# First batch of an attention and maxout kernel: key sums with ones as stationary operand, agent values divided on VectorE, product evacuated by VectorE, fillers moved

## The chip, the cores and the metric

The kernel runs on one core of one Trainium2 chip. The metric is the device time of one execution in microseconds (us), lower is better. The kernel before takes 467.8 us (median of three runs, 466.63 to 468.07).

## The reference

Agent attention in four batches, then a feed-forward layer with a maximum of three products. For each batch b (12544 rows of 128 channels, 49 agents):

```python
scale = 1.0 / np.sqrt(q.shape[-1])
a2k = softmax(scale * agents @ k.T)     # 49 x 12544, over the keys
agent_v = a2k @ v                       # 49 x 128
q2a = softmax(scale * q @ agents.T)     # 12544 x 49, over the agents
x = q2a @ agent_v
h = np.maximum(np.maximum(x @ w1, x @ w2), x @ w3)   # 768 columns
out = h @ w_out
```

The inputs are float32 in HBM, and the output is float32, 50176 x 128.

## The kernel before

The product of agent_v with the weights (w2 - w1, w3 - w1 and so on) is taken once per batch and kept as G, so a slice of 1024 query rows needs only its exps e_q and G. Slices and the k groups of the next batch are interleaved over 49 steps. The first batch has no slices to hide behind: its twelve groups of k and v (ten of nine tiles of 128 rows, two of four) are read, turned (transposed on TensorE), scored and summed by themselves. Evacuating means copying a result of TensorE out of the memory that it writes to (the tiles `uv_ps`, `m_ps` and `o_ps`); a hidden tile is 128 of the 768 hidden columns for one slice. `C31` and `C21` are the places in G where the parts for w3 - w1 and w2 - w1 begin. Every operation is put down with a key, `at(key, ...)`, and is emitted in the order of the keys, so the order of each engine is fixed by hand. The kernel also runs *fillers*, matmuls whose result nobody uses, to keep TensorE busy.

The parts that the change touches (cuts marked):

```python
    def keep_busy(times):                                   # a block of fillers
        t = small_tile("m_ps")
        for _ in range(times):
            nc.tensor.matmul(t, ident, busy, start=True, stop=True, skip_group_check=True)
    # ... in k_group(b, t0, n, key, s); early = first batch
        def values():
            t, c = (d["pair"][:, 1, :], 0) if early else (d["s"], CV)
            for j in range(n):
                e = d["e"][:, j, :A] if early else d["e"][:, j * A:(j + 1) * A]
                nc.tensor.matmul(t[:, c:c + A], d["vb"][:, j, :], e, start=(early and j == 0),
                                 stop=True, skip_group_check=True)

        def key_sums():                                     # exps stationary, one column of ones moving
            for j in range(n):
                for h in range(2):
                    nc.tensor.matmul(d["pair"][h * H:(h + 1) * H, 1, A:A + 1], d["e"][:, j, :],
                                     ones_bf[:, :1], start=False, stop=True, skip_group_check=True)
    # ... in k_tail: the sums' reciprocal scales G when it is evacuated
        def normalise():
            src = last_tile["v"][:, A:A + 1] if s is None else host[s][:, :1]
            nc.vector.reciprocal(r_ag[:, b:b + 1], src)
    # ... in product(c0, *ends), after the matmuls of a piece
                if s is None and c0 == C31:
                    nc.vector.tensor_scalar_mul(G[b][:, a:z], src, r_ag[:, b:b + 1])
                else:
                    nc.scalar.activation(G[b][:, a:z], src, AF.Copy, scale=r_ag[:, b:b + 1])
    # ... in q_group, first slice
            at(last_key + 0.76, turn_q, ("qt", 0), (), "om", [("qe", 0)])
            at(last_key + 0.77, evacuate, ("qe", 0), [("qt", 0)])
            at(last_key + 0.96, scores, ("s", 0), [("qe", 0)], "om", [("ex", 0)])
            at(last_key + 0.97, exps, ("ex", 0), [("s", 0)])
    # ... where the first batch's groups are put down
        if 4 <= g < len(first_sizes) - 2:
            fillers += [(first_key + 6.0 * g + 0.55, 3), (first_key + 6.0 * g + 1.3, 3)]
    k_tail(0, last_key, (last_key + 0.95, last_key + 1.02), None)
    for key, n in fillers + [(KEY["u3"] + 0.05, 2)]:
        at(key, lambda n=n: keep_busy(n), ("busy", key), (), "om", [("busy", key)])
```

The softmax here doesn't subtract the row's maximum and nothing guards it: scores larger than these inputs give would overflow.

## Time and profile before

| | |
|---|---|
| median of the runs | 467.8 us |
| span of the profiled execution | 466.1 us, mean granted clock 0.993 |
| TensorE busy | 442.2 us (95%) |
| VectorE, ScalarE busy | 402.3 (86%), 397.2 us (85%) |
| first batch (loads, scores, values) | 0 to about 44 us |
| thin stretch with the halved clock | about 46 to 53 us |
| steady part | about 66 us to the end |

The prediction shows the lines. In them PE is TensorE's matmuls and PEld its weight loads, DVE is VectorE, ACT ScalarE, POOL GpSimd. A row of the chain of waits reads: start, length, what ended the wait.

### The profile page before, as it was taken

The numbers are of one execution on the slowest core, as the hardware profiler recorded it, in microseconds if no ns is written. First come the engines' busy times: TensorE is split into PE (matmuls) and PEld (weight loads), VectorE is DVE, ScalarE is ACT, GpSimd is POOL, SyncE is SP. The second block draws the span as 40 slices with busy tenths as digits, with TensorE's granted clock in tenths as the row PEclk, the third lists the DMA queues.
The fourth block names the chain that finished last, engine by engine and source line by source line (L and its number), as shares of the span: only waits on it lengthen the run. The fifth ranks groups of instructions, "written<-read, shape, count | busy, mean of one in ns | idle before, by whom it ended". The sixth has DMA issues, their size and how long they took to land.

```text
span 466.1 us, 13549 instructions
## 1 busy us (share of the span) xinstructions
PE 442.2 (95%) x5566; PEld 277.8 (60%) x5573; DVE 402.3 (86%) x514; ACT 397.2 (85%) x461; POOL 171.4 (37%) x179
## 2 busy tenths in 40 slices
PE   2598999999999999999999999999999999999996
PEld 2576456666665666666656766666656555555554
DVE  4254689999989999999989999999988999999995
ACT  3364788999999989899898899998999999999992
POOL 3245855364353453644362536444150010100000
PEclk9999799999999999999999999999999999999999
DMA  8999999998999999996998999996946668643222
GB/s 321 408 409 393 410 336 303 272 342 177 315 302 259 300 323 299 319 293 146 300 334 304 275 310 304 278 295 169 186 125 176 165 167 164 170 136 112 71 85 98
DMA packets 81449, 118.26 MB, mean 254 GB/s; under 512 B 55207, under 2 KB 56683, under 8 KB 81387
## 3 DMA queue, kind: packets, MB, share of 16 engines
q1 hardware_dynamic: 81184, 117.30, 84.0%
q8 instruction: 43, 0.70, 0.6%
q14 instruction: 19, 0.16, 0.1%
q10 hardware_dynamic: 203, 0.10, 0.1%
HBM read 78.74 MB, written 25.69 MB: 224 GB/s over the span
## 4 chain that ended last, share of the span: by engine, by line
PE 84%; DVE 5%; ACT 4%; DMA 4%; issue 2%; SPq 0%; POOL 0%; DVEq 0%; ACTq 0%; POOLq 0%
PE uv_ps L544 34%; PE o_ps L583 28%; PE o_ps L574 6%; DVE r L569 4%; PE m_ps L497 4%; PE m_ps L518 3%; ACT a_sb L559 3%; DMA st<-in_k_dram 2%; PE m_ps L257 2%; DMA st<-in_v_dram 2%; PE m_ps L332 1%; PE m_ps L315 1%; PE uv_ps L297 1%; PE m_ps L532 1%; PE uv_ps L338 1%
## 5 line engine op out<-in xcount | busy, mean ns | idle before, releaser
L569 DVE TENSOR_TENSOR r<-uv_ps,a_sb 128x1024 bf16<-128x1024 f32 x245 | 297.1, 1219 | 16.0 <-PE uv_ps L544 6.2
L559 ACT ACTIVATE a_sb<-uv_ps 128x1024 bf16<-128x1024 f32 x245 | 240.8, 1027 | 14.4 <-PE uv_ps L544 12.9
L544 PE MATMUL uv_ps<-e_q,G 49*128 49x512 bf16 (+3 forms) x1248 | 187.9, 370 | 2.7 <-DVE r L569 0.6
L583 PE MATMUL o_ps<-wo_bf,r 128*128 128x128 bf16 x2352 | 175.3, 220 | 0.2 <-DVE r L569 0.2
L583 PEld LDWEIGHTS <-r 128*128 128x128 bf16 x2352 | 137.8, 98 | 40.0 <-issue 38.1
L544 PEld LDWEIGHTS <-G 49*128 49x128 bf16 x1248 | 57.8, 94 | 65.3 <-issue 32.9
L358 POOL TENSOR_TENSOR Eacc<-Eacc,e_k 128x441 f32<-128x441 f32 (+1 forms) x30 | 30.5, 1015 | 132.6 <-ACT e_k L326 132.6
L590 DVE TENSOR_TENSOR o_sb<-o_ps,recips 128x512 f32<-128x512 f32 x98 | 67.4, 688 | 8.9 <-PE o_ps L583 6.3
L492 POOL CAST q_bf<-st 128x1024 bf16<-128x1024 f32 x49 | 50.8, 1040 | 60.8 <-DMA qT<-q_bf 59.5
L567 ACT ACTIVATE r<-uv_ps 128x1024 bf16<-128x1024 f32 x49 | 50.1, 1023 | 17.7 <-PE uv_ps L544 17.4
L283 POOL CAST k_bf<-st 128x1152 bf16<-128x1152 f32 (+2 forms) x45 | 50.5, 1122 | 27.5 <-DMA st<-in_k_dram 24.9
L556 ACT ACTIVATE uv_ps<-uv_ps 128x1024 f32<-128x1024 f32 x49 | 49.6, 1012 | 2.6 <-PE uv_ps L544 2.4
L574 PE MATMUL o_ps<-G,e_q 128*128 128x256 bf16 x196 | 38.0, 276 | 0.6 <-DVE o_sb L590 0.6
L290 POOL CAST v_bf<-st 128x1152 bf16<-128x1152 f32 (+1 forms) x33 | 37.4, 1134 | 0.7 <-DMA st<-in_v_dram 0.3
L524 ACT ACTIVATE e_q<-m_ps 128x512 bf16<-128x512 f32 x49 | 29.8, 607 | 1.4 <-PE m_ps L518 1.4
L303 DVE COPY kT<-uv_ps 128x1152 bf16<-128x1152 bf16 (+1 forms) x15 | 10.7, 712 | 18.1 <-PE uv_ps L297 18.0
L574 PEld LDWEIGHTS <-e_q 128*128 128x128 bf16 x196 | 12.5, 97 | 19.3 <-issue 17.8
L288 ACT ACTIVATE v_bf<-st 128x1152 bf16<-128x1152 f32 (+1 forms) x12 | 12.8, 1070 | 13.0 <-DMA st<-in_v_dram 12.9
L497 PEld LDWEIGHTS <-q_bf 128*128 128x128 bf16 x264 | 15.3, 99 | 12.9 <-issue 11.6
L503 DVE COPY qT<-m_ps 128x1024 bf16<-128x1024 bf16 (+1 forms) x33 | 22.2, 672 | 0.8 <-PE m_ps L497 0.8
L497 PE MATMUL m_ps<-ident,q_bf 128*128 128x128 bf16 x264 | 20.9, 223 | 0.0
L518 PE MATMUL m_ps<-qT,agT 128*64 128x512 bf16 (+3 forms) x104 | 19.9, 388 | 0.0
(73 smaller groups left out, 219.9 us busy)
## 6 DMA issues: line engine op xcount, KB each, us to landing
st<-in_q_dram SPq DMA_DIRECT2D x46, 512.0 KB, 4.8
out_dram<-o_sb SPq DMA_DIRECT2D x46, 512.0 KB, 3.5
st<-in_k_dram SPq DMA_DIRECT2D x40, 576.0 KB, 6.0
st<-in_v_dram SPq DMA_DIRECT2D x40, 576.0 KB, 7.1
st<-in_k_dram SPq DMA_DIRECT2D x3, 512.0 KB, 6.0
st<-in_v_dram SPq DMA_DIRECT2D x3, 512.0 KB, 6.8
wst<-in_moe_w_dram SPq DMA_DIRECT2D x3, 384.0 KB, 10.4
st<-in_q_dram SPq DMA_DIRECT2D x2, 384.0 KB, 4.2
```

Of the source, the lines that this page charges most:

```text
L283: nc.gpsimd.tensor_copy(out=d["kb"][:, :n, :], in_=d["k"][:, :n, :])
L290: nc.gpsimd.tensor_copy(out=d["vb"][:, :n, :], in_=d["v"][:, :n, :])
L492: nc.gpsimd.tensor_copy(out=d["qb"], in_=d["q"])
L497: nc.tensor.transpose(t[:, j * P:(j + 1) * P], d["qb"][:, j, :], ident)
L544: nc.tensor.matmul(t[:, h, j0 * P:j1 * P], G[b][h * H:h * H + A, col + f * P:col + (f + 1) * P], d["e"][h * H:h * H + A, j0 * P:j1 * P], s ...
L556: nc.scalar.activation(u, u, AF.Relu)
L559: nc.scalar.activation(a_sb[f], u, AF.Relu)
L567: nc.scalar.activation(r, v_ps[f], AF.Relu)
L569: nc.vector.tensor_tensor(out=r, in0=v_ps[f], in1=a_sb[f], op=ALU.max)
L574: nc.tensor.matmul(t[:, i * 2 * C:(i + 1) * 2 * C], d["e"][:, jj * P:(jj + 1) * P], G[batch[jj]][:, C1O:C1O + 2 * C], start=(i == 0), stop ...
L583: nc.tensor.matmul(t[:, c:c + C], r_sb[f][:, h, jj * P:(jj + 1) * P], wo_bf[:, f, :], start=False, stop=True, skip_group_check=True)
L590: nc.vector.tensor_tensor(out=d["out"][:, j:j + m, :], in0=d["o", o].rearrange("p (j c) -> p j c", c=C), in1=d["r"][:, j:j + m].unsqueeze( ...
```

## The change

Its intent is to shorten the ramp ahead of the steady part. The sums of the exps come from a matmul with ones as stationary operand and the exps moving, so every partition holds the sum of each agent in one row of 49; half as many matmuls are needed, and the division can be done once on the agent values (128 x 49) in place of on G. G's pieces are then plain copies, all on VectorE. The scores of the first q slice come ahead of the product. The turn of the next batch's first k group goes behind the second hidden tile. Six fillers near the end of the batch go, and four come in the thin stretch.

```diff
-                last_tile["v"] = d["pair"][:, 1, :]
+                last_tile["t"] = d["s"]
 ...
-                e = d["e"][:, j, :A] if early else d["e"][:, j * A:(j + 1) * A]
+                e = d["e"][:, j * A:(j + 1) * A]
                 nc.tensor.matmul(t[:, c:c + A], d["vb"][:, j, :], e, start=(early and j == 0),
                                  stop=True, skip_group_check=True)
-        def key_sums():
-            (cut: the 2 n one-column matmuls above)
-        def add_sums():
-            (cut)
+                if early:
+                    nc.tensor.matmul(t[:, A:2 * A], ones_bf, e, start=False, stop=True,
+                                     skip_group_check=True)
 ...
-                turn = 6.0 * s - 3.3 if s else KEY["u1"] + 0.01
+                turn = 6.0 * s - 3.3 if s else KEY["v0"] + 0.01
 ...
         def normalise():
-            src = last_tile["v"][:, A:A + 1] if s is None else host[s][:, :1]
-            nc.vector.reciprocal(r_ag[:, b:b + 1], src)
+            if s is None:
+                r = last_tile["t"][:, :A]
+                nc.vector.reciprocal(r, Vacc[b][:, A:])
+                nc.vector.tensor_tensor(out=avT[:, b, :A], in0=Vacc[b][:, :A], in1=r, op=ALU.mult)
+            else:
+                nc.vector.reciprocal(r_ag[:, b:b + 1], host[s][:, :1])
 ...
-                if s is None and c0 == C31:
-                    nc.vector.tensor_scalar_mul(G[b][:, a:z], src, r_ag[:, b:b + 1])
+                if s is None:
+                    nc.vector.tensor_copy(out=G[b][:, a:z], in_=src)
 ...
-            at(last_key + 0.96, scores, ("s", 0), [("qe", 0)], "om", [("ex", 0)])
-            at(last_key + 0.97, exps, ("ex", 0), [("s", 0)])
+            at(last_key + 0.94, scores, ("s", 0), [("qe", 0)], "om", [("ex", 0)])
+            at(last_key + 0.941, exps, ("ex", 0), [("s", 0)])
 ...
-        if 4 <= g < len(first_sizes) - 2:
+        if 4 <= g < len(first_sizes) - 3:
             fillers += [(first_key + 6.0 * g + 0.55, 3), (first_key + 6.0 * g + 1.3, 3)]
 ...
-    for key, n in fillers + [(KEY["u3"] + 0.05, 2)]:
+    for key, n in fillers + [(last_key + 0.9, 2), (KEY["u1"] + 0.01, 2),
+                             (KEY["u3"] + 0.05, 2)]:
```

Cut are the tiles and arguments that follow from it (no ones behind the exps, Vacc 98 columns wide, no scale when the linear part of G is evacuated).

More of the change, by code (lines that the diff above doesn't have):

```diff
@@ L174 @@
     r_ag = const.tile([P, B], FP32, name="r_ag")
-    e_first = [const.tile([P, KT, H], BF16, name=f"e_first{i}") for i in range(3)]
-    for t in e_first:
-        nc.vector.memset(t[:, :, A:], 1.0)
     sel = const.tile([P, 2], BF16, name="sel")
@@ L251, in linear_product_out @@
     def linear_product_out():
-        nc.scalar.activation(G[0][:, C1O:WC], linear["t"][:, C:3 * C], AF.Copy, scale=r_ag[:, 0:1])
+        nc.scalar.activation(G[0][:, C1O:WC], linear["t"][:, C:3 * C], AF.Copy)
     def keep_busy(times):
@@ L318, in exps @@
         def exps():
-            if early:
-                d["e"] = e_first[early_groups.index(t0) % 3]
-                nc.scalar.activation(d["e"][:, :n, :A],
-                                     d["s"][:, :n * A].rearrange("p (j a) -> p j a", a=A), AF.Exp,
-                                     scale=scale)
-                return
             d["e"] = work.tile([P, KT * A], BF16, tag="e_k", bufs=3, name="e_k")
@@ L330, in values @@
             for j in range(n):
-                e = d["e"][:, j, :A] if early else d["e"][:, j * A:(j + 1) * A]
+                e = d["e"][:, j * A:(j + 1) * A]
                 nc.tensor.matmul(t[:, c:c + A], d["vb"][:, j, :], e, start=(early and j == 0),
                                  stop=True, skip_group_check=True)
-        def key_sums():
-            for j in range(n):
-                for h in range(2):
-                    nc.tensor.matmul(d["pair"][h * H:(h + 1) * H, 1, A:A + 1], d["e"][:, j, :],
-                                     ones_bf[:, :1], start=False, stop=True, skip_group_check=True)
-        def add_sums():
-            src = d["pair"][:, 1, A:A + 1]
-            nc.vector.tensor_tensor(out=src, in0=src, in1=Vacc[b][:, A:], op=ALU.add)
+                if early:
+                    nc.tensor.matmul(t[:, A:2 * A], ones_bf, e, start=False, stop=True,
+                                     skip_group_check=True)
         def add_values():
-            w = A + 1 if early else A
+            w = 2 * A if early else A
             src = d["pair"][:, 1, :w] if early else d["s"][:, CV:CV + A]
-            if t0 + n == NT:
-                nc.vector.tensor_tensor(out=avT[:, b, :A], in0=src[:, :A], in1=Vacc[b][:, :A], op=ALU.add)
+            if t0 + n == NT and not early:
+                nc.vector.tensor_tensor(out=avT[:, b, :A], in0=src, in1=Vacc[b], op=ALU.add)
             elif t0:
@@ L378, in k_group @@
             at(min(key + 13.2, done), values, ("kv", g), [("ke", g)])
-            at(min(key + 13.2, done), key_sums, ("kn", g), [("kv", g)])
-            at(min(key + 13.6, done + 0.01), add_values, ("ka", g), [("kv", g), ("kn", g)])
-            if t0 + n == NT:
-                at(done + 0.02, add_sums, "sums0", [("ka", g)])
+            at(min(key + 13.6, done + 0.01), add_values, ("ka", g), [("kv", g)])
         else:
@@ L445, in k_tail @@
         at(sum_key + 0.81, normalise, ("normalise", b),
-           ["sums0"] if s is None else [("total", s), ("ka", s - 1)])
+           [("ka", ("early", NT - last_size))] if s is None else [("total", s), ("ka", s - 1)])
         pieces = ((C31, C31 + 2 * P, C1O) if s is None else (C31, WC), (C21, C31))
@@ L672 @@
     last_size = first_sizes[-1]
-    early_groups = [sum(first_sizes[:g]) for g in range(len(first_sizes))]
     at(first_key - 35, prep, "prep", (), "om", ["prep"])
```

## The prediction

> **What bounds the kernel now.** I read the page first, for the share of each engine and the strip of slices.
>
> ```profile
> PE 442.2 (95%) x5566; PEld 277.8 (60%) x5573; DVE 402.3 (86%) x514; ACT 397.2 (85%) x461; POOL 171.4 (37%) x179
> ...
> PE   2598999999999999999999999999999999999996
> ...
> PEclk9999799999999999999999999999999999999999
> ```
>
> TensorE is the bound, and its row is full from slice 3 on. Only the first slices have holes, and the granted clock dips in one of them (slice 4, 46.6 to 58.3 us). Next I cut the span into stretches with the table of windows (columns: length, busy time with count for PE, PEld, DVE, ACT, POOL, then clock, DMA share, GB/s).
>
> ```profile
> 26.00:42.00 16.00, 15.74 (x328) 12.00 (x330) 8.24 (x16) 9.43 (x14) 7.13 (x7) 1.00 1.04 398
> 42.00:44.50 2.50, 1.77 (x48) 1.48 (x42) 1.01 (x4) 0.73 (x3) 0.85 (x1) 1.00 1.03 410
> 44.50:47.00 2.50, 1.52 (x12) 0.73 (x13) 1.57 (x4) 1.05 (x3) 2.20 (x3) 0.85 1.01 406
> 47.00:50.00 3.00, 2.65 (x15) 1.24 (x16) 0.82 (x2) 2.71 (x3) 2.91 (x4) 0.50 1.03 409
> 50.00:54.00 4.00, 3.87 (x36) 1.98 (x36) 2.58 (x3) 1.78 (x3) 3.22 (x4) 0.61 1.02 409
> ...
> 66.00:400.00 334.00, 332.45 (x4189) 208.34 (x4188) 312.56 (x384) 307.28 (x357) 138.13 (x142) 1.00 0.92 258
> ```
>
> From 66 us PE is busy 332.45 of 334: nothing to gain there without taking PE work away. The order of instructions of both kernels, compared with line numbers stripped, is the same after about 62 us. So the change can only move the date at which the steady part starts. Before that date, 26 to 42 us is full of PE work, part of it fillers (matmuls whose result nobody uses) and all beside a saturated DMA (398 to 410 GB/s); 42 to 54 us is a thin stretch in which the clock falls to 0.50. The chain of waits shows what is serial there.
>
> ```profile
> 41.74 0.38 PE uv_ps L338 x18
> 42.12 0.32 PE uv_ps L315 x8
> 42.44 0.33 ACT e_first L321
> ...
> 43.29 0.57 PE m_ps L497 x8
> ...
> 43.88 0.33 DVE qT L503
> ...
> 44.26 0.22 DVE avT L349
> ...
> 44.91 0.18 DVE r_ag L418
> ...
> 45.18 0.49 DVE G L437
> ...
> 46.38 0.61 ACT e_q L524
> ...
> 48.06 1.08 PE uv_ps L297 x9
> ```
>
> The end of the first batch runs scores, exps, values, agent values (avT), reciprocal, product into G, then the first slice's exps (e_q) and hidden matmuls. The last row is nine transposes in 1.08 us; the same nine took 0.50 us at 37.41. That is the halved clock.
>
> **What the Trainium skill says.** (1) "TensorE: Matmul & The Clock Gate", Part 1, "The HAM clock gate": the clock is 1.2 GHz by default and 2.4 GHz after a busy window of about 3.4 us, and falls back after an idle one; the windows run freely. The trace agrees on the ratio (1.08 against 0.50 us) and roughly on the time: it is slow from about 46.2 to 53 us, 6.8 us, or two windows. It also shows that a thin stretch is enough: PE was 61% busy in 44.5 to 47. (2) Same page, "Back-to-back issue gap": start to start never under about 25 ns however small N is. Nine values matmuls of 49 columns take 0.23 us in the chain, 25.6 ns each; but the 18 one-column ones take 0.38 us, 21 ns each, slightly under it. So a one-column matmul costs nearly what a 49-column one does. (3) "VectorE: DVE Perf Modes", "First, the fixed hardware budget": reciprocal repeats a divide step 8 times. That might mean 8 cycles per element; the groups by shape say less.
>
> ```profile
> L538 DVE RECIPROCAL recips<-m_ps 128x8 f32<-128x8 f32 x49 | 9.7, 197 | 0.1
> L418 DVE RECIPROCAL r_ag<-m_ps 128x1 f32<-128x1 f32 x3 | 0.5, 168 | 3.4 <-PE m_ps L413 3.4
> ```
>
> Seven more elements cost 29 ns, 4.1 ns each, so 49 elements should take about 0.168 + 48 x 0.0041 = 0.37 us.
>
> **The change part by part.**
>
> Key sums. Removed: 18 matmuls of one column per group of nine tiles (0.38 us). Added: nine of 49 columns with ones stationary (estimate 0.23 us, as for the values). Saved: 0.15 us per group, 0.15 x 98/9 = 1.6 us over the batch. It all lies on PE, which is the chain from 21 us to 42 us, but only as far as data have arrived (below).
>
> Fillers before the end of the batch. The group ten from the start loses its two blocks of three: 0.22 + 0.38 at 37.9 and 0.75 at 39.38 in the chain, 1.35 us of PE time. With the sums, PE could finish some 2.4 us sooner from 26 us on.
>
> How far data allow it. POOL's casts wait for loads:
>
> ```profile
> 38.96 0.61 POOL L283 CAST k_bf<-st 128x512 bf16<-128x512 f32 x1 [0.71 <-DMA st<-in_k_dram]
> 40.90 1.04 POOL L492 CAST q_bf<-st 128x1024 bf16<-128x1024 f32 x1 [1.33 <-DMA st<-in_q_dram]
> ```
>
> The last k group is ready at 39.57 and the first q slice at 41.94. PE turns q between the last two values groups, in program order, at 43.29 now; it cannot before about 42.0. DMA is saturated, so these dates don't move. So of the 2.4 us, about 1.25 us survive: qT's evacuation starts at 42.6 in place of 43.88.
>
> The division. Before: avT sum (0.21) starts at 44.26, then sum column and reciprocal (0.17 each) run beside the product matmul; G's evacuation starts 0.92 us after avT started. After: sum (about 0.26 for 98 columns), reciprocal 0.37, multiply 0.21, each waiting for the one ahead (0.03 to 0.24 us a hop, as between 44.26 and 44.91), then matmul and start of evacuation, about 0.35. Sum 1.25 to 1.6: longer by 0.3 to 0.7 us. So G's first piece ends at 44.8 to 45.3 in place of 45.66.
>
> The exps of q move ahead of the product (they now end near 44.7, before 46.99), so they leave the chain. But the hidden matmuls still stand behind all product matmuls on PE (about 1.2 us after G's first piece), so they start near 46.1, 0.9 us sooner than 47.03.
>
> Product evacuated by VectorE: ACT loses 0.90 us (46.98) which stood ahead of the first relu, so relu starts when the first hidden matmul is done, 46.6 in place of 47.78. VectorE gains about 0.48, 0.75 and 1.02 (slope 0.27 us per 256 columns), where it had idled 2.26 us.
>
> Turning k behind the second hidden tile and four more fillers (two ahead of q's scores, two after the first two hidden tiles, 0.43 us a pair at full clock, 0.85 at half): if the clock stays up, transposes, hidden tiles and q's turn save about 2 us of PE time between 47 and 52; the relus then bind and the fourth hidden tile starts at 49.2 rather than 51.5. Gain 2.3 us. If the clock still drops, the fillers cost nearly what they fill, and the gain shrinks to 0.3 to 0.8 us.
>
> I can't tell which. The change also thins PE at 40 to 45 us (data-bound, fillers gone): by my timetable it is busy for about half of 40.3 to 45.2. I give a full clock 45%. Mean: 0.45 x 2.3 + 0.55 x 0.6 = 1.4 us, so 467.8 - 1.4 = 466.4.
>
> **The rivals.** (a) The clock drops earlier, at 43 us, because the batch's end is thinner: the chain of serial hops at half clock gives all the lead back, 467.5 to 468.2. For it: 61% busy was too little before. Against: two fillers stand in the hole. (b) VectorE becomes the bound of the first slices: its three copies take 2.25 us in a row and the second hidden half waits for the third. For it: that wait is new. Against: ACT needs until 48.5 for two relus anyway. It costs under 1 us: about 466. (c) The lead is lost later, to loads for the next batch: DMA share is 1.02 until 62 us. Against: casts run 3 us or more ahead of the transposes that use them. Then 467.5. (d) All works and the clock stays up: 465.
>
> **Range and chances.** (d) and (a) set the ends, with 0.5 us for the scatter of the runs before (466.63 to 468.07): 464.6 to 468.2. 2% would be 9.4 us, four times the best case: faster 0.01, slower 0.01, same 0.98.
>
> **What the profile after would show.** Nine values and nine sums in about 0.46 us in the chain; qT's evacuation near 42.6; the 49-wide reciprocal near 0.37 us; the first relu near 46.6; and PE fuller and nine transposes in 0.5 us at 47 to 52 (d) or 1.1 us (a). From 66 us to the end, the same length as before within 0.5 us. I am wrong if the steady part changes length, if the last q load lands at another time, or if the clock behaves in a third way.

## The result, and the profile after

The changed kernel takes 464.55 us (median of four executions, 464.44 to 464.77). The ratio to the kernel before is 0.9936, 95% interval 0.9919 to 0.9953: same by the limit of 2%, but clearly 0.6% faster. The four executions of the kernel before in that comparison took 466.63 to 468.07; the experiments below have 33 more. A ratio is the mean time of one kernel's fast runs over that of the other's of the same rounds, so it is not quite the ratio of the medians.

The strip of the page after, as before: the dip of the clock in slice 4 is gone.

```profile
PE 438.5 (95%) x5473; PEld 274.3 (59%) x5473; DVE 402.8 (87%) x512; ACT 396.5 (86%) x460; POOL 171.1 (37%) x179
...
PE   2597899999999999999999999999999999999995
...
PEclk9999999999999999999999999999999999999999
```

The table of windows after, same columns as in the prediction:

```profile
42.00:44.50 2.50, 1.58 (x21) 0.85 (x19) 1.64 (x5) 1.15 (x2) 0.80 (x1) 1.00 1.02 410
44.50:47.00 2.50, 2.26 (x17) 0.78 (x16) 1.61 (x3) 1.33 (x3) 2.18 (x3) 1.00 1.02 407
47.00:50.00 3.00, 2.52 (x34) 1.63 (x33) 2.30 (x3) 1.69 (x3) 2.94 (x4) 1.00 1.02 410
50.00:54.00 4.00, 3.51 (x39) 1.69 (x39) 3.31 (x6) 3.91 (x6) 3.19 (x4) 1.00 1.03 409
66.00:400.00 334.00, 332.96 (x4178) 207.91 (x4175) 312.43 (x386) 307.60 (x357) 136.90 (x142) 1.00 0.88 260
```

From 44.5 to 47 TensorE is busy for 2.26 us of 2.5 in place of 1.52, and the clock stays at 1.00 in all stretches. The steady part looks as before.

The chain of waits after (start, length, what):

```profile
40.64 1.05 POOL q_bf L478
...
41.74 0.64 PE m_ps L483 x8
...
42.40 0.44 DVE qT L489
...
44.13 0.43 DVE G L423
...
45.80 0.39 PE uv_ps L530 x2
...
47.06 0.62 PE uv_ps L294 x9
```

Its start is new: GpSimd's cast of the first q slice, which waited for the load, has taken the place of TensorE's backlog. Nine transposes take 0.62 us in place of 1.08. Point by point:

| event | before | after | gain |
|---|---|---|---|
| q's load has landed, cast starts | 40.90 | 40.64 | 0.26 |
| evacuation of qT starts | 43.88 | 42.40 | 1.48 |
| first piece of G done | 45.66 | 44.55 | 1.11 |
| first hidden matmuls start | 47.03 | 45.28 | 1.75 |
| first relu starts | 47.78 | 45.71 | 2.07 |
| in-place relu of the fourth hidden tile starts | 52.13 | 48.96 | 3.17 |
| first output scaled | 64.91 | 61.71 | 3.20 |
| end | 466.1 | 462.7 | 3.4 |

Nearly all is won by 52 us and kept. From the first scaled output to the end it is 401.2 us before and 401.0 after.

### The profile page after: what moved, and what is told of

Same layout as the page of the kernel before. It is cut to its first block, busy times and chain, and to the rows that moved or that the text cites. A ratio compares the mean times of both kernels' runs of the same rounds, so it can differ in the third digit from the quotient of the medians.

```text
span 462.7 us, 13350 instructions
## 1 busy us (share of the span) xinstructions
PE 438.5 (95%) x5473; PEld 274.3 (59%) x5473; DVE 402.8 (87%) x512; ACT 396.5 (86%) x460; POOL 171.1 (37%) x179
## 4 chain that ended last, share of the span: by engine, by line
PE 80%; DMA 8%; DVE 5%; ACT 4%; issue 1%; SPq 0%; POOL 0%; DVEq 0%; ACTq 0%
PE uv_ps L530 34%; PE o_ps L569 29%; PE o_ps L560 6%; DMA st<-in_k_dram 5%; PE m_ps L483 4%; DVE r L555 4%; PE m_ps L504 3%; ACT a_sb L545 2%; DMA st<-in_q_dram 2%; DMA st<-in_v_dram 2%; PE m_ps L323 2%; PE m_ps L312 1%; PE m_ps L518 1%; DVE o_sb L576 1%; ACT e_q L510 0%
```

## The experiments

Twelve kernels ran, each five rounds and a profiled execution (six executions); the kernel before, 33 in all. All gave correct results. "Full" counts executions whose mean granted clock over the whole span was 0.996 or more. What lies between 0.996 and 1.000 is not the thin stretch in the traces that we have: e0's, at 0.997, shows 1.00 up to 460 us and 0.61 from there, where the last work of TensorE ends. The last two columns are a ruler from the one trace of each: from the start of q's cast (so the landing of q's load, which varies between 40.33 and 41.38, is taken out) to the first scaled output, and from there to the end.

| run | edit | median (lowest to highest) | full | q cast to first output | to the end |
|---|---|---|---|---|---|
| before | | 467.39 to 467.58 in the three calls (465.93 to 469.3) | 18 of 33 | 24.01 | 401.2 |
| after, first runs | whole change | 464.55 (464.44 to 464.77) | 4 of 4 | 21.07 | 401.0 |
| e0 | whole change | 464.63 (464.38 to 465.73) | 6 of 6 | 21.08 | 401.1 |
| e1 | less the new fillers | 465.96 (464.53 to 467.45) | 1 of 6 | 23.73 | 400.8 |
| e2 | before, new fillers alone | 466.65 (466.03 to 467.62) | 6 of 6 | 24.03 | 401.2 |
| e7 | sums and division alone | 466.90 (465.10 to 468.31) | 2 of 6 | 21.39 | 401.1 |
| e11 | sums, division, new fillers | 465.17 (464.58 to 466.46) | 5 of 6 | 21.40 | 401.4 |
| e3 | second piece of G by ScalarE | 464.96 (464.47 to 465.46) | 6 of 6 | 21.23 | 401.1 |
| e4 | turn of k early again | 465.10 (464.59 to 465.59) | 6 of 6 | 21.11 | 401.4 |
| e5 | old fillers kept | 464.64 (464.21 to 464.74) | 6 of 6 | 21.09 | 401.1 |
| e6 | before, old fillers dropped | 467.18 (465.73 to 468.41) | 1 of 6 | 23.08 | 401.1 |
| e8 | values ahead of q's turn | 464.55 (463.45 to 465.37) | 6 of 6 | 20.42 | 401.3 |
| e9 | e8, one old filler pair less | 464.24 (463.65 to 465.34) | 5 of 6 | 20.49 | 400.8 |
| e10 | e9, q's cast split | 464.06 (463.79 to 464.74) | 5 of 6 | 20.57 | 400.8 |

The executions of the kernel before fall in groups by their own mean clock: 14 at 0.998 or 0.999 take 466.6 us on average (median 466.4), 11 at 0.991 take 468.4, and 8 between them 467.4. So a full dip costs about 1.8 us. By this reckoning the kernel before has one in a third of its executions and perhaps part of one in another quarter; only one trace of it was kept, so where the clock fell in the others is not shown. The average of all 33 is 467.4, 0.8 above the full-clock ones. The ten executions of the changed kernel (first runs and e0) average 464.7. The gain is thus about 1.9 us at equal clock and about 0.8 us of dips that no longer come, 2.7 us together.

### e0: the change again

```diff
(none)
```

> The changed kernel once more, as the yardstick for the runs beside it. Both theories: 464.5 us (464.2 to 465.0), clock near 1.00. If some of its executions show a clock near 0.99 and take 466 us or more, the full clock in its first trace was luck of the phase.

Measured 464.63 us, all six executions at 0.997 or more. The full clock in the first trace was no luck. One execution at 0.999 took 465.73; no trace shows why.

### e1: without the new fillers

```diff
-    for key, n in fillers + [(last_key + 0.9, 2), (KEY["u1"] + 0.01, 2),
-                             (KEY["u3"] + 0.05, 2)]:
+    for key, n in fillers + [(KEY["u3"] + 0.05, 2)]:
```

> The changed kernel without its two new pairs of fillers (4 matmuls of 512 columns, about 0.9 us of TensorE at full clock). Theory 'clock': without them the clock falls again near 43 to 47 us and stays low for two windows; time 466.0 to 467.2, mean clock about 0.99. Rival 'dates': the gain is the removed work and the new order; time 464.2 to 464.8, as less TensorE work is left.

Measured 465.96 us; the one execution at 0.999 took 464.53, as the whole change does, the others 464.86 to 467.45 at 0.989 to 0.995. The table of windows of its profiled execution:

```profile
42.00:44.50 2.50, 1.03 (x17) 0.68 (x16) 1.70 (x5) 1.19 (x2) 1.15 (x1) 1.00 1.02 406
44.50:47.00 2.50, 1.89 (x16) 0.57 (x13) 1.55 (x2) 1.59 (x2) 2.35 (x3) 0.75 1.03 409
47.00:50.00 3.00, 2.78 (x20) 2.04 (x21) 1.91 (x3) 0.34 (x1) 2.92 (x4) 0.50 1.02 409
50.00:54.00 4.00, 3.88 (x41) 2.07 (x40) 2.01 (x3) 3.30 (x4) 3.21 (x4) 0.50 1.03 408
54.00:58.00 4.00, 3.82 (x29) 1.26 (x28) 3.64 (x5) 3.42 (x6) 2.91 (x5) 0.75 1.02 411
```

TensorE is busy 1.03 us from 42 to 44.5 in place of 1.58, and then the clock falls to 0.50. It stays there from about 45.8 to 56 us, 10.2 us, where it was 6.8 us in the trace before. Four matmuls without a use are worth 1.3 us on average, all of it through the clock as far as one execution can show: the one at full clock without them took neither more nor less. 'Clock' is confirmed; its range, from 466.0, is missed by 0.04 us, and the low stretch is longer than it forecast.

### e2: the new fillers alone

```diff
+    for key, n in fillers + [(last_key + 0.9, 2), (KEY["u1"] + 0.01, 2),
+                             (KEY["u3"] + 0.05, 2)]:
-    for key, n in fillers + [(KEY["u3"] + 0.05, 2)]:
```

> The kernel before with only the two new pairs of fillers added. Theory 'clock': the clock stays full at 46 to 53 us and 1.2 to 2.0 us are gained: 465.8 to 466.6. Rival 'dates': nothing is gained, 467.6 to 468.4, as the fillers add 0.9 us to TensorE.

Measured 466.65 us, all executions at 0.996 or more: the dips are gone, as 'clock' says (0.05 above its range), and 466.65 is what the kernel before takes at full clock. The gain in the same rounds is 0.15% with an interval that includes none (0.9964 to 1.0006). Half of its executions took 466.0 to 466.2 and the others 467.1 to 467.6. The profiled one is of the second kind, and its casts on GpSimd show where that came from:

```profile
20.86 1.15 POOL L283 CAST k_bf<-st 128x1152 bf16<-128x1152 f32 x1 [5.93 <-DMA st<-in_k_dram]
```

The same cast in the kernel before:

```profile
19.86 1.15 POOL L283 CAST k_bf<-st 128x1152 bf16<-128x1152 f32 x1 [4.65 <-DMA st<-in_k_dram]
```

One load came 1 us later, and q's turn then starts at 44.34 in place of 43.22, although q itself had landed at 40.39. With the old sums TensorE works off a backlog from 21 us to the end of the batch, so a late load at 20 us was not made good in this trace.

### e7: sums and division alone

```diff
(shortened: the change, with fillers, turn of k, order of q's scores as before, and)
+                if s is None and c0 == C31:
+                    nc.vector.tensor_copy(out=G[b][:, a:z], in_=src)
+                elif s is None:
+                    nc.scalar.activation(G[b][:, a:z], src, AF.Copy)
```

> Only the new key sums with the division on VectorE: product's second part evacuated by ScalarE, fillers, turn of k and order of q's scores as before. Theory 'clock': lead of about 0.15 us x 7 groups at the end of the batch, less 0.3 us for the longer division, and the clock still falls: 467.0 to 467.6. Rival 'dates': the sums are the larger part of the gain: 465.5 to 466.5.

Measured 466.90 us: above the rival's range and 0.1 below the theory's. The two full executions took 465.10 and 465.91, the three at 0.988 or 0.989 took 467.5 to 468.3. Its trace is of a full one: q's turn at 41.94, when the cast ended at 41.89. The turn follows the values matmuls without a gap, so the sums alone bring TensorE's own work level with q's load (with the old fillers dropped too, it waits 0.56 us for the cast in the changed kernel). At full clock that is most of the gain; but without new fillers the clock fell in four of six executions, and hides it. That this is more often than before rests on e1, e6 and e7 together (14 of 18, against 15 of 33 in the kernel before); e7 alone does not show it. The expectation had the size of the lead right and its worth too low.

### e11: sums, division and new fillers

```diff
(e7, with the new fillers)
```

> The new sums and division (as in e7) and the two new pairs of fillers, nothing else. Theory 'data limit and clock': those two carry nearly all of the gain: 464.9 to 465.4 in every execution, mean clock 0.997 or more. Rival: VectorE's evacuation, the later turn of k or the order of q's scores carry a large part, or keep the clock up: 466 or more, or executions near 467 at 0.99.

Measured 465.17 us, 5 of 6 at full clock, those five 465.08 on average. Of the 1.9 us at equal clock (466.6 to 464.7) the sums carry 1.5. By the ruler 0.33 us is left for all other parts (21.40 against 21.07). The theory holds for the median; of the single executions, one at 0.994 took 466.46, and one at 1.000 took 464.58, less than it allowed.

### e3: second piece of G on ScalarE

```diff
+                if s is None and c0 == C31:
+                    nc.vector.tensor_copy(out=G[b][:, a:z], in_=src)
+                elif s is None:
+                    nc.scalar.activation(G[b][:, a:z], src, AF.Copy)
-                if s is None:
-                    nc.vector.tensor_copy(out=G[b][:, a:z], in_=src)
```

> The changed kernel with the product's second part (768 columns) evacuated by ScalarE again. Theory: it stands ahead of the first relu (0.9 us from about 45.4), so the relus start near 46.3 in place of 45.71 and 0.4 to 0.7 us are lost: 464.9 to 465.3. Rival: the relus are not on the chain, or VectorE's copy costs as much elsewhere: 464.3 to 464.7.

Measured 464.96 us, against 464.64 of e5, which by its own result below is as good as the whole change; by the ruler 0.16 us. ScalarE in time order:

```profile
45.28 0.81 ACT L425 ACTIVATE G<-uv_ps 128x768 bf16<-128x768 f32 x1 [0.84 <-PE uv_ps L418]
...
45.99 1.94 ACT L547 ACTIVATE a_sb<-uv_ps 128x1024 bf16<-128x1024 f32 x2
```

The relu starts at 45.99, only 0.28 us later than in the changed kernel (45.71), where it waits for the first hidden matmuls. A small part of the gain, at the low end of the range expected (464.9).

### e4: turn of k early

```diff
-                turn = 6.0 * s - 3.3 if s else KEY["v0"] + 0.01
+                turn = 6.0 * s - 3.3 if s else KEY["u1"] + 0.01
```

> The changed kernel with the turn of the next batch's k back ahead of the second hidden tile. Theory: the turn then takes the product's second buffer (free at 46.6) and the second hidden tile that of the first relu (46.7), so the two only change places: 464.4 to 464.9. Rival: the relus or VectorE's maximum wait longer: 465.2 or more.

Measured 465.10 us, above the theory's range and below the rival's. The trace shows no loss ahead of the first output (21.11 against 21.07); from there to the end it takes 401.4 in place of 401.0 to 401.1, but e8 shows 401.3 without this edit, and e7, which turns k early too, 401.1. So whether the order of the turn costs anything stays open.

### e5 and e6: the old fillers near the end of the batch

```diff
e5, in the changed kernel:
-        if 4 <= g < len(first_sizes) - 3:
+        if 4 <= g < len(first_sizes) - 2:
e6, in the kernel before:
-        if 4 <= g < len(first_sizes) - 2:
+        if 4 <= g < len(first_sizes) - 3:
```

> The changed kernel with the two blocks of three fillers of the tenth group put back (1.35 us of TensorE). Theory 'data limit': with the new sums TensorE already waits for k and q, so q's turn still starts at about 41.8 and the time stays 464.4 to 464.9, full clock. Rival 'TensorE backlog': the fillers are on the chain and cost up to 1.3 us: 465.5 to 466.

Measured 464.64 us. The cast and turn of q in its trace:

```profile
40.42 1.04 POOL L478 CAST q_bf<-st 128x1024 bf16<-128x1024 f32 x1 [1.38 <-DMA st<-in_q_dram]
...
41.54 0.27 PE L483 MATMUL m_ps<-ident,q_bf 128*128 128x128 bf16 x2
```

With 1.35 us more work on TensorE the turn still starts 0.08 us after the cast. It follows the values without a gap, as in e7, so TensorE's work and the load are just level. Dropping those fillers is worth nothing once the sums have changed.

> The kernel before with only these two blocks of three fillers taken out. Theory 'data limit': TensorE's backlog at the end of the batch shrinks by 1.35 us and q's turn moves from 43.2 to about 42: executions with full clock take 465.1 to 465.6, those with a dip (mean clock 0.99) about 467; median 465.8 to 466.8. Rival: the lead needs the new sums; full-clock executions stay at 466.4 or above.

Measured 467.18 us, ratio 1.000. In the kernel before, dropping them takes most of TensorE's backlog away (q's turn starts 0.48 us after the cast has ended, in place of 1.28; the one execution at 0.996 took 465.73), and the clock takes it back: five of six executions are at 0.985 to 0.993. The table of windows:

```profile
42.00:44.50 2.50, 1.74 (x39) 1.36 (x35) 1.04 (x5) 1.04 (x3) 0.80 (x2) 0.89 1.02 411
44.50:47.00 2.50, 1.74 (x12) 0.83 (x9) 1.44 (x4) 0.62 (x2) 2.19 (x3) 0.50 1.03 406
```

The dip now starts before 44.5, at about 43.9, and lasts 6.8 us again. The expectation of a median under 466.8 was too good: a dip was not an even chance here.

### e8, e9, e10: what binds now

The three edits below are shortened. If q's load sets the chain, work that does not need q should be done while it is awaited. e8 puts the last values, sum, reciprocal and multiply ahead of q's turn, and the product's first part ahead of q's scores. e9 also takes away the last old pair of fillers. e10 also casts q half on GpSimd and half on VectorE, and has ScalarE alone evacuate it.

```diff
e8, in the changed kernel:
-            at(last_key + 0.76, turn_q, ("qt", 0), (), "om", [("qe", 0)])
-            at(last_key + 0.77, evacuate, ("qe", 0), [("qt", 0)])
-            at(last_key + 0.94, scores, ("s", 0), [("qe", 0)], "om", [("ex", 0)])
-            at(last_key + 0.941, exps, ("ex", 0), [("s", 0)])
+            at(last_key + 0.805, turn_q, ("qt", 0), (), "om", [("qe", 0)])
+            at(last_key + 0.815, evacuate, ("qe", 0), [("qt", 0)])
+            at(last_key + 0.96, scores, ("s", 0), [("qe", 0)], "om", [("ex", 0)])
+            at(last_key + 0.97, exps, ("ex", 0), [("s", 0)])
e9, in e8:
-                             (KEY["u3"] + 0.05, 2)]:
e10, in e9 (first slice only):
-            nc.gpsimd.tensor_copy(out=d["qb"], in_=d["q"])
+            nc.gpsimd.tensor_copy(out=d["qb"][:, :n // 2, :], in_=d["q"][:, :n // 2, :])
+            nc.vector.tensor_copy(out=d["qb"][:, n // 2:, :], in_=d["q"][:, n // 2:, :])  # key last_key + 0.705
-            (qT: half on VectorE, then half on ScalarE)
+            nc.scalar.activation(qT, d["qT_ps"], AF.Copy)
```

> The changed kernel with q's turn behind the last values (which had stood behind it) and the product's first part ahead of q's scores. Theory: the last sum, reciprocal and multiply run while TensorE waits for q, so the first piece of G ends near 43.4 in place of 44.55 and the three copies follow it; the hidden tiles then wait for q's exps (near 44.9) in place of 45.28: 463.6 to 464.2. Rival: the chain through q's turn, evacuations, scores and exps is as long, so nothing or under 0.2 us: 464.3 to 464.7. If the clock dips: 465.5 or more.

> As e8 (values ahead of q's turn, product's first part ahead of q's scores), less the last pair of fillers, which stood ahead of the second q turn and of the fourth hidden tile while ScalarE was idle for 1.1 us: that tile starts 0.4 us sooner. Theory: 463.7 to 464.3 with full clock. Rival: the pair kept the clock up: some executions at 465.5 or more with mean clock below 0.996.

> As e9, and the first q slice is cast half on GpSimd and half on VectorE (0.5 us less from its landing to its turn) and evacuated by ScalarE alone. Theory: q's landing sets the chain, so q's exps end 0.5 us sooner and 0.2 to 0.5 us of it reach the end: 463.3 to 464.0. Rival: the product and its three copies on VectorE set the date by then: as e9.

Measured 464.55, 464.24 and 464.06 us. By the ruler e8 is 0.65 us shorter than the change (20.42 against 21.07), which is what the theory said; but the median lies in the rival's range. In its trace (464.70 us) the late landing of q, at 41.17, hides the lead; for the other executions, which spread from 463.45 to 465.37, no trace shows why. e9 adds nothing by the ruler (20.49; one of its executions fell to 0.994 and took 465.34, just short of what the rival said): the second q turn, which the fillers stood ahead of, starts at 47.09 there, when GpSimd's cast of that slice has ended. In e10 the half of the cast on VectorE came late, because it stood behind a sum:

```profile
41.33 0.62 POOL L479 CAST q_bf<-st 128x512 bf16<-128x512 f32 x1 [1.30 <-DMA st<-in_q_dram]
41.99 0.26 DVE L335 TENSOR_TENSOR Vacc<-uv_ps,Vacc 128x98 f32<-128x98 f32 x1 [0.68 <-PE uv_ps L326]
...
42.17 0.42 DVE L482 CAST q_bf<-st 128x512 bf16<-128x512 f32 x1
```

GpSimd's half was done at 41.95, VectorE's at 42.59, no sooner than one cast of 1.04 us would have been (42.37). So the split was not tested fairly, and the rival stands by the ruler (20.57). The 18 executions of e8 to e10 average 464.4 us, against 464.6 of the 16 of the first runs, e0 and e5. That is in favour of the new order, but 0.05% is not settled by these rounds.

## Why the prediction was right or wrong

**Class and place.** Right: the steady part kept its length (401.2 and 401.0 us from the first output to the end), the change acted on the ramp alone, and nothing near 2% was to be had. By the ratio the changed kernel comes to 0.9936 x 467.8 = 464.8, inside the range; the first median, 464.55, is 0.05 below its low end. So the gain was underrated: 1.4 us forecast, 3.0 to 3.25 measured (2.7 against all 33 executions). That the time lies near the range at all is owed to rival (d), which set its low end; taken at its word, 465 less 0.5, that end would have been 464.5.

**Sums.** Right in size. In the trace after, nine values and nine sums start from 37.17 to 37.61, 26 ns apart, so about 0.46 us together as forecast.

**Data limit.** Right, and the heart of the lead: q's turn started at 41.74 (about 42.0 forecast) and waited for the cast; qT's evacuation at 42.40 (42.6). One step of it was wrong: the six dropped fillers were counted into the lead, and e5 shows that they carry none of it once the sums have changed. The prediction also held that loads do not move, and named another landing of q as a sign of being wrong. q landed 0.26 us sooner, but its landing scatters by 1 us between the profiled executions, so this says nothing of the change.

**Division.** The sum was right: from the last sum's start (42.73) to the start of G's first evacuation (44.13) 1.40 us, with 1.25 to 1.6 forecast. A term was not: the 49-wide reciprocal took 0.47 us, not 0.37.

```profile
L401 DVE RECIPROCAL uv_ps<-Vacc 128x49 f32<-128x49 f32 x1 | 0.5, 471 | 0.0
```

**Product and relu.** Mis-sized. The hidden matmuls were put 1.2 us behind G's first piece, from the trace before, in which part of those product matmuls ran at half clock; they came 0.73 us behind (45.28 in place of 46.1), and the relu at 45.71 in place of 46.6. The matmuls of the fourth hidden tile, forecast at 49.2, started at 48.48. The evacuation by VectorE, to which the prediction put down the relu's lead, moves it by only 0.28 us (e3).

**Clock.** The step that set the size. The mechanism was right (e1, e2), and so was its worth, 1.8 us a dip; the chance was not. "I give a full clock 45%" rested on TensorE being half busy from 40.3 to 45.2 us; it was busy 3.06 of 4.90 us there, 62%, and kept its clock. The reading that 61% had been too little was not sound either: that stretch, 44.5 to 47, has the fall at 46.2 inside it. (A smaller slip: TensorE's row of the strip is not full in slice 3, which has an 8.) The runs put the chance of a full clock at 55 of 58 executions of kernels with the new fillers, and at 4 of 18 of those without them that have fewer sums or fewer old fillers (e1, e6, e7). The prediction also took the one trace before as the kernel before; it has a full clock in 18 of 33 executions, so the comparison was with a mixture. The forecast of 2.3 us with the clock up was counted from that trace, with its dip; from trace to trace it came to 3.4. At equal full clock the gain is 1.9 us, for which there was no forecast; and with a dip, where 0.3 to 0.8 was forecast, the three executions of e1 at 0.989 to 0.993 average 466.9, 1.5 us below the dipping ones of the kernel before (e1 lacks the fillers, so that is the nearest case, not the same).

**Rivals.** (a) did not come with the fillers; without them the traces of e1 and e6 show the earlier dip, though from 45.8 and 43.9 us, and e7's executions at 0.988 and 0.989 took about the time that it named. (b) came as a wait and not as a cost: the weights of the second hidden half were loaded at 46.66, when VectorE's third copy had ended, but two fillers ran meanwhile, and e3, which takes a copy back, is no faster. (c) did not come: the lead was 3.17 us at the fourth hidden tile and 3.20 at the first output. (d) came, 0.5 us further down.

What stays open: why e4's median is 0.5 us up, why a few full-clock executions take 1 us more (e0, e11 and the kernel before have some; the late load of e2 is one case that a trace shows), and what the order of q's scores is worth alone, which no run undid by itself.

## What to carry to other kernels

When an engine works off a backlog beside a saturated DMA, work taken from it is gained only until it waits for data; find that date from the casts and loads before adding up the savings, and then look for work that can be done while waiting. Thinning TensorE next to a serial stretch can cost more through its clock than it saves, so read the mean clock of every execution, not one trace, and compare executions of equal clock; a few fillers in the hole can be worth nearly as much as the work removed (here 1.3 us, e1, against 1.5 for the sums). A ruler between two events of the trace, behind the load that scatters, tells apart changes of a few tenths of a us that medians do not (it gave 21.07 and 21.08 for the same kernel); it is still one trace of each.

## What the Trainium skill lacked or had wrong

- "TensorE: Matmul & The Clock Gate", Part 1: it names idle windows and frequent short idles as what lowers the clock, and gives no busy share at which it falls. Here it fell at 46.2 us after 3.4 us with TensorE 63% busy (2.13 us from 42.8, trace before), and stayed up through 3.4 us with 59% (2.02 us from 41.0, trace after), so the share alone does not decide. Once fallen it stayed at half for 6.8 us (before, e6) or 10.2 us (e1). Whether it falls varies between executions of one kernel (15 of 33 below a mean of 0.996), as free-running windows would let one expect. No page says that a few fillers keep it up (four matmuls: from 1 of 6 to 6 of 6 executions at full clock, e1 and e0).
- Same page, which warns that clock events in traces can be unreliable, but has no such case: the granted clock in the trace is shown as 1.00 from 10 to 21 us, where nine transposes take 1.14 us, as they do at 48.00 us at a granted 0.50, against 0.67 from 26 us on. So TensorE's slow start does not appear in that column or in the mean clock.
- Same page, "Back-to-back issue gap": one-column matmuls with 64-column weights came 21 ns apart, under the floor of about 25 ns. They wrote the two halves of the output partitions in turn, and no run here separates that from their width. 49-column ones with two stationary operands in turn (v and ones, 128 columns each, loaded anew each time) came 26 ns apart.
- "VectorE: DVE Perf Modes": no time for the reciprocal. Measured 168 ns for one element per partition, 197 for 8 and 471 for 49; 6.3 ns an element between the first and the last.
